# Two tiles' small products in one chain: grouping transposes, values and scores by kind

## The chip, the cores and the metric

The kernel runs on one core of a Trainium2 chip. The metric is the device time of one execution in microseconds, taken as the median of several runs. The profile tells of one profiled execution. Engines are called as the profile calls them: PE (TensorE, matmuls; PEld its weight loads), DVE (VectorE), ACT (ScalarE), POOL (GpSimd) and SP (SyncE, here a queue that issues transfers).

## The reference

Windowed attention with block summaries, and behind it an expert layer with a softmax gate and a layer norm. Cut to what matters:

```python
# q, k, v: 4 batches, 8 heads, 768 positions, 64 wide; blocks of 32, window 16
k_sum = k.reshape(B, H, nb, block, D).max(axis=3)
v_sum = v.reshape(B, H, nb, block, D).mean(axis=3)
scores_l = scale * q @ k.T                      # kept where |pos - pos'| < 16
scores_s = scale * q @ k_sum.T + log(block)
a = softmax(concat(masked scores_l, scores_s))
attn = a @ concat(v, v_sum)

x = attn as 3072 rows x 512
h = x @ w_in                                    # 512 x 1024
solu = h * softmax(h)
ln = (solu - mean) / sqrt(var + 1e-6) * g_ln
out = ln @ w_out                                # 1024 x 512
```

Everything is 32-bit. The two large products are made exact enough by splitting both operands into a high and a low part and adding three products of the parts.

## The kernel before, in words

The 3072 rows are 24 tiles of 128 rows (`NT`); tile `t` has two large products. `first(t)` makes h: 4 chunks of the contraction, two halves of 512 columns and three products each are 24 matmuls with 512 columns (line 706), into two PSUM banks that every tile from the third on uses again. `second(t)` makes o: 8 chunks and three products, 24 matmuls (line 784). Between the two the row statistics are made: the maximum (DVE, line 716), the exponential (ACT, 721), the product that reads h for the last time (DVE, 729), centring (737, 739 or 741), the sum of squares (ACT, 744) and the root (POOL, 748 to 756).

The attention before it is done in 24 steps, one for 4 heads (two of the four pairs of heads) and 256 positions; two steps, an even one and the odd one after it, make the x rows that two tiles read. Three kinds of small product belong to a step, all of them on PE:

- `scores` (S, line 587): 32 matmuls, 64 rows by 64 columns of the array, into PSUM. Ahead of them the keys are copied into windows (`kw`, 568 and 569). Behind them DVE masks and takes maxima (606), ACT takes exponentials with sums (614), and DVE or POOL multiplies by the inverse sum (621).
- `values_turn` (T): 16 transposes (line 642, tile `t`) of the weights `e`, and two copies to SBUF (`at`).
- `values` (V, line 681): 32 matmuls of `at` with the values (`vt`), and a copy and a subtraction that make the parts `xh` and `xl`.

A fourth kind belongs to a tile: `turn` (R), 16 transposes (line 642, tile `lt`) of its normed rows, with two copies (`lh`) and two subtractions (`ll`, line 769), so that `second` can use them as weights. R of tile t is done `LAG` - 1 = 3 tiles after its h, o of tile t is done 4 tiles after.

PSUM buffers: T, S and R (and a rare sum of values) share two slots with the tag `s`; V and o take turns in two banks (`place_x`). SBUF: `at`, `e`, `kw`, `qt`, `vt`, `lh` and `ll` have two buffers each, `he`, the rows of h, five (`NHE`).

The order is made by a planner (`Plan`) while the program is built. Every operation is recorded with its cost, the engines that can do it, and what it depends on through its buffers. `issue` gives each operation a due time, which for PE work is its place in the program, and `order` lists them greedily: the operation that can start first, and of several the one that is due first. It does this 64 times with noise on the due times and keeps the order with the earliest end on PE. Each engine then executes its list in that order. An operation with `then` set holds PE for its successor: nothing comes between.

From tile 6 on (`NEAR`) the main loop chains, in every tile t: T of step t + 3, then R of tile t - 3 together with V of step t + 2, then S of step t + 4. `run` records one or several generators as one operation on PE and lets each record what follows on the other engines. Up to tile 5 the small products are recorded one by one. The head of a chain also waits for what its second member waits for. `load_q`, `load_v` and `load_keys` are recorded at fixed places of the loop; `scored(i)` tells in which tile the scores of step i are made, and from it follows when keys are loaded and their block maxima taken.

Of the kernel before, what the change touches and what calls it, by code (L numbers as in the profile page):

```python
# [11 lines left out]
F32 = mybir.dt.float32  # L12
# [8 lines left out]
P = 128  # L21
# [5 lines left out]
QT = 64  # L27
# [10 lines left out]
NT = B * S // P  # L38
LAG = 4
NHE = 5  # L40
EARLY = 3
MEANS = 2
NEAR = 6
WPT = 2


# [26 lines left out]
class Plan:  # L73
# [41 lines left out]
    def op(self, engine, cost, fn, r=(), w=(), nbytes=0, after=(), alt=(), port=False):  # L115

        deps = set(after)

        def of(table, part):
            for k, v in table.items():
                if part is None or k is None or k == part:
                    deps.update(v)

        o = Op({e: (c, f) for e, c, f in ((engine, cost, fn), *alt)}, deps,
               len(self.ops), nbytes, port)
        r = [x if isinstance(x, tuple) else (x, None) for x in r]
        w = [x if isinstance(x, tuple) else (x, None) for x in w]
        for b, part in r:  # L130
            of(b.writers, part)
        for b, part in w:
            of(b.writers, part)
            of(b.readers, part)
            for p in b.prev:
                deps.update(p.ops)
                p.gone = True
        assert not any(b.gone for b, _ in r + w)
        for b, part in r:
            b.readers.setdefault(part, []).append(o)  # L140
            b.ops.append(o)
        for b, part in w:
            b.writers.setdefault(part, []).append(o)
            b.ops.append(o)
        deps.discard(o)
        self.ops.append(o)
        return o
# [115 lines left out]
def attn_then_solu(ctx: ExitStack, tc: tile.TileContext, q, k, v, vr, vb, w_in, w_out, g_ln, out):  # L263
# [3 lines left out]
    nc = tc.nc  # L267
    plan = Plan()
    op = plan.op
    pe, act, dve, pool, sp = "pe", "act", "dve", "pool", "sp"  # L270
# [12 lines left out]
    sb = ctx.enter_context(tc.tile_pool(name="sb", bufs=1))  # L283
# [150 lines left out]
    def load_keys(b, p, after=()):  # L434
        pp, i = divmod(p, 2)
        if i == 0:
            kraw[b, pp] = plan.buf(sb, [P, 2, SP], F32, "kraw", 3, f"kraw{b}_{pp}")
        x = kraw[b, pp]
        op(sp, 0.43, lambda: nc.sync.dma_start(out=x.ap[:, i], in_=k[b, pp, :, i]), w=[(x, i)], nbytes=P * SP * 4,
           after=after)  # L440

    def key_blocks(b, p):
        pp, i = divmod(p, 2)
        x = kraw[b, pp]
        if i == 0:
            ksum[b, pp] = plan.buf(sb, [P, 2, NB], F32, "ksum", 3, f"ksum{b}_{pp}")
        y = ksum[b, pp]
        op(dve, 0.87, lambda: nc.vector.tensor_reduce(
            out=y.ap[:, i], in_=x.ap[:, i, HALO:HALO + S].rearrange("p (n j) -> p n j", j=BLOCK),
            op=ALU.max, axis=AX.X), r=[(x, i)], w=[(y, i)])  # L450
# [82 lines left out]
    def load_q(b, g, pairs=None, after=()):  # L533
        if (b, g) not in qt:
            qt[b, g] = plan.buf(sb, [P, NPAIR, G * QT], F32, "qt", 2, f"qt{b}_{g}")
        x = qt[b, g]
        part = slice(None) if pairs is None else slice(2 * pairs, 2 * pairs + 2)
        op(sp, 0.43, lambda: nc.sync.dma_start(out=x.ap[:, part], in_=q[b, g, :, part]),
           w=[x] if pairs is None else [(x, 2 * pairs), (x, 2 * pairs + 1)],
           nbytes=P * 4096 if pairs is None else P * 2048, after=after)  # L540
# [81 lines left out]
           lambda: z.ap.rearrange("p (u o) -> p u o", o=1).broadcast_to([P, 8, KC]), r=[z], w=[e], port=True)  # L622
        es[b, g, pp] = e

    def run(*parts):

        mine = [x for x in ((f, next(f, None)) for f in parts) if x[1]]
        if mine:
            cost, fns, r, w = zip(*(x for _, x in mine))
            op(pe, sum(cost) - 0.25 * (len(mine) - 1), lambda: [f() for f in fns],  # L630
               r=[x for y in r for x in y], w=[x for y in w for x in y])
            done = plan.ops[-1]
        for f, _ in mine:
            assert next(f, None) is None
        return done if mine else None

# [7 lines left out]
    def values_turn(b, g, pp):  # L644
        nm_ = f"{b}_{g}_{pp}"
        e = es.pop((b, g, pp))

        tp = plan.buf(ps, [P, 2, 8, QT], F32, "s", 2, f"t{nm_}")
        yield 0.82, lambda: turn_halves(tp.ap[:KC], lambda n: e.ap[:, n, :]), [e], [tp]
        at = plan.buf(sb, [P, 2, 8, QT], F32, "at", 2, f"at{nm_}")  # L650
        for cu in range(2):
            copy(COPY_P, lambda cu=cu: at.ap[:KC, cu], lambda cu=cu: tp.ap[:KC, cu], r=[(tp, cu)], w=[(at, cu)])
        ats[b, g, pp] = at
# [105 lines left out]
    def turn(t):  # L759

        e = cen.pop(t)
        hi = plan.buf(sb, [P, NFC, P], F32R, "lh", 2, f"lh{t}")
        lo = plan.buf(sb, [P, NFC, P], F32R, "ll", 2, f"ll{t}")
        tp = plan.buf(ps, [P, 2, NFC, QT], F32, "s", 2, f"lt{t}")
        yield 0.85, lambda: turn_halves(tp.ap, lambda f: e.ap[:, f * P:(f + 1) * P]), [e], [tp]
        for r in range(2):
            part = lambda x, r=r: x.ap[:, :, r * QT:(r + 1) * QT]
            copy(COPY_P, lambda part=part: part(hi), lambda r=r: tp.ap[:, r], r=[(tp, r)], w=[(hi, r)])
            op(dve, 0.6, lambda part=part, r=r: nc.vector.tensor_tensor(  # L769
                out=part(lo), in0=tp.ap[:, r], in1=part(hi).bitcast(F32), op=ALU.subtract),  # L770
               r=[(tp, r), (hi, r)], w=[(lo, r)])
        lnT[t] = hi, lo
# [24 lines left out]
    its = [(b, g) for b in range(B) for g in range(NG)]  # L797
# [20 lines left out]
    for i in range(2 * NKC):  # L818
        split_w_in(*divmod(i, 2))
        if i % 2 == 0 and i < 2 * NPP:  # L820
            run(values_turn(0, 0, i // 2))
            run(values(0, 0, i // 2, 0, True))
# [6 lines left out]
        load_w(2 * NKC + f, w_out[f * P:(f + 1) * P, :])  # L829
    rows = [(hh, i) for hh in range(2) for i in range(2)]  # L830

    scored = lambda i: i - 2 if i - 2 < NEAR else max(NEAR - 1, i - 4)

    load_at, blocks_at = {}, {}
    for later in range(1, B):
        for p in range(NPAIR):
            t = scored(2 * NG * later + p // 2)
            old = 2 * NG * (later - 1) + (2 * NG - 2 if p > 1 else -1)
            free = scored(old) + (old - 2 >= NEAR) if old > 1 else 0
            load_at[later, p] = max(t - (3, 2, 2, 2)[p], free)  # L840
            blocks_at[later, p] = max(t - (2, 1, 2, 1)[p], load_at[later, p])

    def pairs(at, t):
        return [x for x in at if at[x] == t]

    step = lambda i: (*its[i // 2], i % 2)
    for t in range(NT):
        n, j = divmod(t, 2)
        b, g = its[n]
        near = t >= NEAR  # L850
        if not near:
            run(scores(*step(t + 2)))

        if t == NEAR - 1 or (near and j == 0 and n + 3 < len(its)):
            load_q(*its[n + 3])
        elif j == 0 and not near:
            load_q(*its[n + 2], after=begun if n == 0 else ())
        if j == 0 and n + 2 < len(its):
            load_v(*its[n + 2], after=begun if n == 0 else ())
        for p in pairs(load_at, t):  # L860
            load_keys(*p, begun if t < 4 else ())
        first(t)
        rows_behind = [turn(t - LAG + 1)] if t > LAG - 2 else []
        if near:
            parts = [run(values_turn(*step(t + 3)))] if t + 3 < NT else []
            parts.append(run(*rows_behind, *([values(*step(t + 2))] if t + 2 < NT else [])))
            if t + 4 < NT:
                parts.append(run(scores(*step(t + 4))))


            for x, y in zip(parts, parts[1:]):
                x.then = y
                y.deps.add(x)
            parts[0].deps.update(*[y.deps - {parts[0]} for y in parts[1:2]])
        else:
            run(*rows_behind)
        for f in range(WPT * t, min(WPT * t + WPT, NFC)):
            split_w_out(f)
        if t > LAG - 1:
            second(t - LAG)  # L880
        if not near:
            run(values_turn(*step(t + 2)))
            if t == NEAR - 1:
                run(scores(*step(t + 3)))
            run(values(*step(t + 2), t))
            if t == NEAR - 1:
                run(values_turn(*step(t + 3)))
                run(scores(*step(t + 4)))
        for p in pairs(blocks_at, t):
            key_blocks(*p)  # L890
        if t == MEANS:
            mean_values_pe(1)
        if 0 < b < B - 1 and g < 2:
            add_rows(b + 1, *rows[2 * g + j])
            if g == j == 1:
                mean_values(b + 1)
        if j == 1 and n + 2 < len(its):
            load_v2(*its[n + 2])
    for t in range(NT - LAG + 1, NT):
        run(turn(t))  # L900
        second(t - 1)
    second(NT - 1)

    def idle(x):
# [49 lines left out]
```

## Time and profile before

| | |
|---|---|
| median of 3 runs | 393.17 us (392.65 to 394.0) |
| span of the profiled execution | 392.1 us |
| PE busy | 383.5 us, 98% |
| PE weight loads | 298.3 us, 76% |
| DVE busy | 275.7 us, 70% |
| ACT busy | 248.7 us, 63% |
| POOL busy | 99.2 us, 25% |
| HBM read, written | 40.11 MB, 6.29 MB |

The page gives no whole-execution time for the profiled execution beside its span; the runs' median lies 1.07 us above the span. Times are from the first to the last instruction. Matmuls overlap: each large one is shown with about 0.39 us, but they start 0.23 us apart. So the rate of PE is read from starts, not from durations.

### The profile page before, as it was taken

To read this page: it belongs to the slowest core of one execution; us is meant where nothing else is said; L and a number is where in the kernel's file an instruction comes from. 1 tells how busy PE (TensorE), PEld (TensorE's weight loads), DVE (VectorE), ACT (ScalarE), POOL (GpSimd) and SP (SyncE) were. 2 spreads that over 40 slices of the span, in tenths; PEclk is the share of its full clock that TensorE was granted. 3 is DMA by queue.
4 is the path that set the end of the run, shared out by engine and by line. 5 is a ranking of instruction groups with operands and counts; after the bars stand their busy time and mean duration, and the time that the engine had idled before them with its cause. 6 is when DMAs were issued, how large, how long until landed. Compare 5 with 4: busy or idle time off the path is not lost.

```text
span 392.1 us, 9677 instructions
## 1 busy us (share of the span) xinstructions
PE 383.5 (98%) x3697; PEld 298.3 (76%) x3703; DVE 275.7 (70%) x884; ACT 248.7 (63%) x746; POOL 99.2 (25%) x245
## 2 busy tenths in 40 slices
PE   8999998999999999999999999999999999999996
PEld 3535766667878888878888888888888888888786
DVE  4999998999889877577767657667658664554330
ACT  3889686999798846657548557468467363533411
POOL 4325011515854421237220121220121021101100
PEclk9999999999999999999999999999999999999999
DMA  7999992136269230363330320330310000000011
GB/s 286 417 419 382 353 367 89 57 109 176 84 218 238 89 134 2 125 188 112 106 131 2 138 80 27 144 87 28 107 49 28 3 28 27 13 16 28 28 55 54
DMA packets 14994, 49.24 MB, mean 126 GB/s; under 512 B 1836, under 2 KB 2092, under 8 KB 13412
## 3 DMA queue, kind: packets, MB, share of 16 engines
q1 hardware_dynamic: 11084, 41.89, 30.8%
q10 hardware_dynamic: 3864, 6.74, 4.6%
q8 instruction: 29, 0.48, 0.5%
q14 instruction: 17, 0.14, 0.1%
HBM read 40.11 MB, written 6.29 MB: 118 GB/s over the span
## 4 chain that ended last, share of the span: by engine, by line
PE 81%; DMA 7%; DVE 6%; ACT 3%; issue 1%; ACTq 1%; SPq 0%; DVEq 0%
PE o L784 35%; PE h L706 29%; PE x L681 5%; PE s L587 4%; PE lt L642 3%; PE t L642 3%; DMA raw<-in_w_in 3%; DMA g_sb<-in_g_ln 2%; DMA vt<-vsum 1%; DMA qt<-in_q 1%; DVE e L606 1%; DVE cv L388 1%; DVE he L729 1%; ACT at L289 1%; DVE cv L296 1%
## 5 line engine op out<-in xcount | busy, mean ns | idle before, releaser
L784 PE MATMUL o<-w,lh 128*128 128x512 f32 (+1 forms) x400 | 127.2, 388 | 0.1
L706 PE MATMUL h<-w,xh 128*128 128x512 f32 x384 | 125.5, 394 | 0.4 <-DVE he L729 0.4
L614 ACT ACTIVATE e<-e,nm 128x120 f32<-128x120 f32 x192 | 73.1, 385 | 25.1 <-DVE nm L606 25.0
L784 PEld LDWEIGHTS o<-w,lh 128*128 128x128 f32 x400 | 74.1, 188 | 17.6 <-issue 2.4
L706 PEld LDWEIGHTS h<-w,xh 128*128 128x128 f32 x384 | 72.1, 188 | 17.5 <-ACT e L614 0.8
L784 PE MATMUL o<-w,ll 128*128 128x512 f32 (+1 forms) x200 | 76.4, 382 | 0.0
L706 PE MATMUL h<-w,xl 128*128 128x512 f32 x192 | 74.8, 390 | 0.0
L716 DVE TENSOR_REDUCE hm<-h 128x1 f32<-128x512 f32 x48 | 32.6, 686 | 40.4 <-PE h L706 40.4
L289 ACT COPY at<-t 120x512 f32<-120x512 f32 x46 | 24.8, 585 | 43.9 <-PE t L642 43.4
L784 PEld LDWEIGHTS o<-w,ll 128*128 128x128 f32 x200 | 37.7, 188 | 6.3
L706 PEld LDWEIGHTS h<-w,xl 128*128 128x128 f32 x192 | 36.0, 188 | 7.0
L606 DVE CUSTOM_DVE_ANT_0 e<-s,mask 128x120 f32<-128x120 f32 x192 | 40.6, 278 | 0.4 <-PE s L587 0.4
L721 ACT ACTIVATE he<-h,hm 128x512 f32<-128x512 f32 x48 | 32.8, 694 | 9.8 <-DVE hm L718 9.8
L614 ACT ACTIVATION_READ_ACCUMULATOR e<-e,nm 128x1 f32 x192 | 36.6, 191 | 0.0
L769 DVE TENSOR_TENSOR ll<-lt,lh 128x512 fp32r<-128x512 f32 x48 | 31.9, 683 | 5.8 <-ACT lh L289 5.6
L748 POOL TENSOR_SCALAR ss<-ss 128x1 f32<-128x1 f32 x24 | 7.1, 297 | 112.4 <-ACT sq L744 112.3
L729 DVE SCALAR_TENSOR_TENSOR he<-h,hz,he 128x512 f32<-128x512 f32 x48 | 34.1, 746 | 0.4
L681 PE MATMUL x<-at,vt 120*64 120x64 f32 (+1 forms) x768 | 28.3, 225 | 1.6 <-ACT at L289 1.6
L681 PEld LDWEIGHTS x<-at,vt 120*64 120x64 f32 (+1 forms) x768 | 24.6, 137 | 6.4 <-ACT at L289 2.9
L296 DVE TENSOR_TENSOR e<-e,z 128x960 f32<-128x960 f32 x23 | 26.6, 1156 | 0.5
L289 ACT CAST lh<-lt 128x512 fp32r<-128x512 f32 x33 | 18.6, 596 | 12.7 <-PE lt L642 9.7
L291 POOL COPY kw<-ksum 128x192 f32<-128x192 f32 x21 | 9.3, 445 | 65.8 <-PE s L587 33.4
(94 smaller groups left out, 519.0 us busy)
## 6 DMA issues: line engine op xcount, KB each, us to landing
vt<-in_v SPq DMA_DIRECT2D x12, 1024.0 KB, 5.4
kraw<-in_k SPq DMA_DIRECT2D x16, 400.0 KB, 9.4
out<-os ACTq DMA_DIRECT2D x23, 256.0 KB, 2.0
qt<-in_q SPq DMA_DIRECT2D x11, 512.0 KB, 5.1
raw<-in_w_in SPq DMA_DIRECT2D x8, 512.0 KB, 10.6
raw<-in_w_out SPq DMA_DIRECT2D x8, 512.0 KB, 9.2
st_v<-in_vr SPq DMA_DIRECT2D x6, 512.0 KB, 12.4
st_v<-in_vb SPq DMA_DIRECT2D x8, 384.0 KB, 3.2
```

What stands on the lines that cost most here:

```text
L289: by = {act: lambda: nc.scalar.copy(out=to(), in_=of()), dve: lambda: nc.vector.tensor_copy(out=to(), in_=of()), pool: lambda: nc.gpsimd.t ...
L296: by = {dve: lambda: nc.vector.tensor_tensor(out=to(), in0=a(), in1=b(), op=kind), pool: lambda: nc.gpsimd.tensor_tensor(out=to(), in0=a() ...
L606: nc.vector.tensor_tensor_reduce(out=e.ap[:, n, :], in0=sc.ap[:, j, (2 * i + up) * KC:(2 * i + up + 1) * KC], in1=mask[:, mi, :], scale=-S ...
L614: nc.scalar.activation(out=e.ap[:, n, :], in_=e.ap[:, n, :], func=AF.Exp, bias=nm.ap[:, n:n + 1], scale=-1.0, accum_out=z.ap[:, n:n + 1])
L642: nc.tensor.transpose(out=to[:, r, n, :], in_=of(n)[rows, :], identity=ident[rows, rows])
L681: nc.tensor.matmul(xp()[j * D:(j + 1) * D, i, qs], vs.ap[:k, u, cs], at.ap[:k, u % 2, n[j] + u // 2, :], start=not apart, stop=not apart o ...
L706: nc.tensor.matmul(hp.ap, a.ap[:, c, ts], w.ap[:, i], start=(c == 0 and n == 0), stop=(c == NKC - 1 and n == 2))
L716: op(dve, 0.6, lambda i=i, hp=hp: nc.vector.tensor_reduce(out=nms.ap[:, i:i + 1], in_=hp.ap, op=ALU.max, axis=AX.X, negate=True), r=[hp], ...
L721: op(act, 0.71, lambda i=i, hp=hp: nc.scalar.activation(out=part(i), in_=hp.ap, func=AF.Exp, bias=nm.ap, accum_out=zs.ap[:, i:i + 1]), r=[ ...
L729: op(dve, 0.67, lambda i=i, hp=hp: nc.vector.scalar_tensor_tensor(out=part(i), in0=hp.ap, scalar=zs.ap[:, 0:1], in1=part(i), op0=ALU.mult, ...
L769: op(dve, 0.6, lambda part=part, r=r: nc.vector.tensor_tensor(out=part(lo), in0=tp.ap[:, r], in1=part(hi).bitcast(F32), op=ALU.subtract), ...
L784: nc.tensor.matmul(o.ap[:, cols], a.ap[:, f, :], w.ap[:, i, cols], start=(f == 0 and n == 0), stop=(f == NFC - 1 and n == 2))
```

## The change

From tile 8 on (`PAIRED`) the small products of two tiles go together.

- In every even tile one chain holds T of steps t + 4 and t + 5, V of steps t + 2 and t + 3, and S of steps t + 6 and t + 7, in this order. Two blocks of one kind follow each other.
- The row transposes R of tiles t - 4 and t - 3 are a chain of two of their own, recorded ahead of `first(t)` of the even tile.
- The second T's copies are recorded after the first V (`rest=False`), and `at` has three buffers.
- At the end of tile 7 the deeper pipeline is filled: T of step 11 and S of steps 12 and 13 are recorded one by one.
- The head of a chain waits for what its first members wait for (two in the pair of R, three in the long chain), and for the PE work behind what the later ones wait for.
- The planner is told 0.25 us less for a block behind one of its kind (`off`).
- `load_q` goes to other places, `scored` changes with the scores, and so the keys of later batches are loaded in other tiles. In the tail the last four tiles' R are two pairs. The scratch for dynamic DMA is set to 8192.

```diff
+PAIRED = 8
...
-    def run(*parts):
+    def run(*parts, rest=True, off=0.0):
...
-            op(pe, sum(cost) - 0.25 * (len(mine) - 1), lambda: [f() for f in fns],
+            op(pe, sum(cost) - 0.25 * (len(mine) - 1) - off, lambda: [f() for f in fns],
                r=[x for y in r for x in y], w=[x for y in w for x in y])
             done = plan.ops[-1]
-        for f, _ in mine:
+        for f, _ in mine if rest else ():
             assert next(f, None) is None
...
-        at = plan.buf(sb, [P, 2, 8, QT], F32, "at", 2, f"at{nm_}")
+        at = plan.buf(sb, [P, 2, 8, QT], F32, "at", 3, f"at{nm_}")
...
-    scored = lambda i: i - 2 if i - 2 < NEAR else max(NEAR - 1, i - 4)
+    def scored(i):
+        if i < PAIRED + 4:
+            return i - 2 if i - 2 < NEAR else max(NEAR - 1, i - 4)
+        return PAIRED - 1 if i < PAIRED + 6 else i // 2 * 2 - 6
...
+    def chain(parts, first=2):
+
+        for x, y in zip(parts, parts[1:]):
+            x.then = y
+            y.deps.add(x)
+        mine = set(parts)
+        for x in parts[1:first]:
+            parts[0].deps.update(x.deps - mine)
+        for x in parts[first:]:
+            for d in x.deps - mine:
+                parts[0].deps.update([y for y in (d, *d.deps) if "pe" in y.can and y not in mine])
+
     for t in range(NT):
...
-        near = t >= NEAR
+        near, paired = t >= NEAR, t >= PAIRED
...
-        if t == NEAR - 1 or (near and j == 0 and n + 3 < len(its)):
+        if paired:
+            if t == PAIRED:
+                load_q(*its[n + 3])
+            if j and n + 4 < len(its):
+                load_q(*its[n + 4])
+        elif t == NEAR - 1 or (near and j == 0 and n + 3 < len(its)):
             load_q(*its[n + 3])
...
+        if paired and j == 0:
+            chain([run(turn(t - LAG)), run(turn(t - LAG + 1), off=0.25)])
         first(t)
-        rows_behind = [turn(t - LAG + 1)] if t > LAG - 2 else []
-        if near:
-            parts = [run(values_turn(*step(t + 3)))] if t + 3 < NT else []
-            parts.append(run(*rows_behind, *([values(*step(t + 2))] if t + 2 < NT else [])))
-            if t + 4 < NT:
+        if not paired:
+            rows_behind = [turn(t - LAG + 1)] if LAG - 2 < t < PAIRED - 1 else []
+            if near:
+                parts = [run(values_turn(*step(t + 3)))]
+                parts.append(run(*rows_behind, values(*step(t + 2))))
                 parts.append(run(scores(*step(t + 4))))
...
+                chain(parts)
+            else:
+                run(*rows_behind)
...
-        if t > LAG - 1:
+        if LAG - 1 < t < NT - 1:
             second(t - LAG)
...
+        if paired and j == 0:
+            parts = []
+            if t + 4 < NT:
+                behind = values_turn(*step(t + 5))
+                parts = [run(values_turn(*step(t + 4))), run(behind, rest=False, off=0.25)]
+            if t + 2 < NT:
+                parts.append(run(values(*step(t + 2))))
+                if t + 4 < NT:
+                    assert next(behind, None) is None
+                parts.append(run(values(*step(t + 3)), off=0.25))
+            if t + 6 < NT:
+                parts += [run(scores(*step(t + i)), off=0.25 * (i - 6)) for i in (6, 7)]
+            chain(parts, 3)
...
+        if t == PAIRED - 1:
+            run(values_turn(*step(t + 4)))
+            for i in (5, 6):
+                run(scores(*step(t + i)))
...
-    for t in range(NT - LAG + 1, NT):
-        run(turn(t))
+    for t in range(NT - LAG, NT, 2):
+        behind = turn(t + 1)
+        chain([run(turn(t)), run(behind, rest=False, off=0.25)])
         second(t - 1)
+        assert next(behind, None) is None
+        second(t)
     second(NT - 1)
...
-    nc = bacc.Bacc("TRN2", target_bir_lowering=False, num_devices=1)
+    nc = bacc.Bacc("TRN2", target_bir_lowering=False, num_devices=1, dynamic_dma_scratch_size=8192)
```

More of the change, by code (lines that the diff above doesn't have):

```diff
@@ L861, in attn_then_solu @@
             load_keys(*p, begun if t < 4 else ())
+        if paired and j == 0:
+            chain([run(turn(t - LAG)), run(turn(t - LAG + 1), off=0.25)])
         first(t)
-        rows_behind = [turn(t - LAG + 1)] if t > LAG - 2 else []
-        if near:
-            parts = [run(values_turn(*step(t + 3)))] if t + 3 < NT else []
-            parts.append(run(*rows_behind, *([values(*step(t + 2))] if t + 2 < NT else [])))
-            if t + 4 < NT:
-                parts.append(run(scores(*step(t + 4))))
[L871 to L876, printed above, removed]
+        if not paired:
[3 more added lines that the diff above has]
+                parts.append(run(*rows_behind, values(*step(t + 2))))
+                parts.append(run(scores(*step(t + 4))))
+                chain(parts)
+            else:
+                run(*rows_behind)
         for f in range(WPT * t, min(WPT * t + WPT, NFC)):
             split_w_out(f)
-        if t > LAG - 1:
+        if LAG - 1 < t < NT - 1:
             second(t - LAG)
```

## The prediction

> **What bounds the kernel now.** I read the page first, then the waits of TensorE, then its instructions in order of time across one steady period.
>
> ```profile
> span 392.1 us, 9677 instructions
> PE 383.5 (98%) x3697; PEld 298.3 (76%) x3703; DVE 275.7 (70%) x884; ACT 248.7 (63%) x746; POOL 99.2 (25%) x245
> PEclk9999999999999999999999999999999999999999
> PE x L681 <- ACT at L289: 1.6, 2, 1.0
> PE h L706 <- DVE he L729: 0.4, 1, 0.4
> ```
>
> TensorE is busy for 98% of the span, no slice falls below nine tenths of the clock, and the longest wait group of PE is 1.6 us in total. No transfer or other engine can give back much here; a gain has to come out of TensorE's own stream. So I read that stream (start, duration, instructions with their count):
>
> ```profile
> 204.30 0.39 PE L706 MATMUL h<-w,xh 128*128 128x512 f32 x1
> 204.62 0.69 PE L642 MATMUL t<-ident,e 64*120 64x64 f32 x16
> 205.15 0.66 PE L642 MATMUL lt<-ident,he 64*128 64x64 f32 x16
> 205.74 1.15 PE L681 MATMUL x<-at,vt 120*64 120x64 f32 x32
> 206.82 1.05 PE L587 MATMUL s<-kw,qt 64*64 64x120 f32 x32
> 207.80 0.50 PE L784 MATMUL o<-w,lh 128*128 128x512 f32 x1
> 208.14 0.40 PE L784 MATMUL o<-w,ll 128*128 128x512 f32 x1
> 208.37 0.62 PE L784 MATMUL o<-w,lh 128*128 128x512 f32 x2
> ...
> 218.90 0.69 PE L642 MATMUL t<-ident,e 64*120 64x64 f32 x16
> ```
>
> This is tile 12, counting the groups of 24 h matmuls. A period runs from 204.62 to 218.90: 14.28 us. The 48 large matmuls follow each other at 0.23 us (208.14 to 208.37; 0.227 over the long stretches), 10.88 us; the remaining 3.40 us are the small products with what their neighbourhood costs. Blocks, from start to the next start: T (values' transposes, t) 0.53, R (row transposes, lt) 0.59, V 1.08, S 0.98. The first large one after them takes 0.34 (207.80 to 208.14) instead of 0.23, with the next two slow as well: 0.13 in all; the step from the last h to T is 0.32 instead of 0.23: 0.09. 0.09 + 0.53 + 0.59 + 1.08 + 0.98 + 0.13 = 3.40.
>
> What a change of kind costs is read from the block's end. Single small matmuls last:
>
> ```profile
> L681 PE MATMUL x<-at,vt 120*64 120x64 f32 x704 | 25.6, 225 | 1.6 <-ACT at L289 1.6
> L587 PE MATMUL s<-kw,qt 64*64 64x120 f32 x704 | 23.1, 269 | 0.4 <-DVE ll L769 0.4
> L642 PE MATMUL t<-ident,e 64*120 64x64 f32 x384 | 16.5, 226 | 0.1
> ```
>
> T's last one starts at 204.62 + 0.69 - 0.23 = 205.08, R's first at 205.15: 0.06 between two blocks of transposes (rounded). V's last starts at 206.66 and S begins at 206.82: 0.15. S's last starts at 207.60, o begins at 207.80: 0.19. Inside blocks the mean step is 0.03. So leaving a block for another shape costs 0.12 (V) or 0.16 (S) over the ordinary step, and a seam between two transposes only 0.03.
>
> **The change, part by part.** The small work itself stays the same; what changes is how often TensorE changes its shape. I add up TensorE's time for everything small from tile 7 on, both ways.
>
> Before: tiles 7 to 19 have a full chain of T, R, V, S: 13 x 3.40 = 44.20. Tile 20 lacks S: 2.42. Tile 21 has R and V, and then R stands alone five times. Two rows give a lone R and a lone T:
>
> ```profile
> 117.28 0.69 PE L642 MATMUL t<-ident,e 64*120 64x64 f32 x16
> 117.89 0.50 PE L784 MATMUL o<-w,lh 128*128 128x512 f32 x1
> ...
> 346.24 0.71 PE L642 MATMUL lt<-ident,he 64*128 64x64 f32 x16
> 346.88 0.50 PE L784 MATMUL o<-w,lh 128*128 128x512 f32 x1
> ```
>
> A lone R costs 0.64 + 0.09 + 0.13 = 0.86, five of them 4.30; tile 21 0.09 + 0.64 + 1.08 + 0.13 = 1.94. Sum before: 52.86.
>
> After, tile 7: its chain has lost R (it waits for the pair at tile 8): 0.09 + 0.62 (lone T) + 1.08 + 0.98 + 0.13 = 2.90. Once, T of step 11 and S of 12 and 13 are issued by themselves to fill the deeper pipeline: 0.62 + 0.22 = 0.84 and 2 x (0.98 + 0.22) = 2.40, together 3.24. Tiles 8, 10, 12, 14, 16: T T V V S S. The T T seam is the one measured; V V and S S stand nowhere in the trace. Bounds: nothing saved (each block as long as today), or the whole of leaving and entering a shape, 0.19 (S's 0.16 plus T's 0.03 slower start: led by h, T takes 0.53; following T, R takes 0.59 with an exit of 0.15 in it against 0.06). I take the excess of leaving, 0.12 for V and 0.16 for S, since the nearest row, the T R seam, shows it nearly gone: 0.09 + 0.53 + 0.59 + (2.16 - 0.12) + (1.96 - 0.16) + 0.13 = 5.18, five times 25.90. Tile 18 (T T V V): 3.38. Tile 20 (V V): 2.26. Ten pairs of row transposes, each 0.09 + 0.53 + 0.59 + 0.13 = 1.34, stand alone: 13.40. Sum after: 51.08. **TensorE's stream becomes 1.78 us shorter.** Of this the steady pair gives 6.80 - 5.18 - 1.34 = 0.28, five times 1.4; the tail and tile 7 give about 1.5, and the three single blocks, dearer alone than in a chain, take about 1.1 back. With nothing saved at V V and S S (seven and five seams, 1.64 us) 0.14 would be left; with 0.19 at all twelve it is 2.4.
>
> [...]
>
> **What hides the rest.** These I cost at nothing, each by its cover. The second T's copies to SBUF must wait until the first V has read its third buffer, and the second S needs the PSUM slot that they free: V + S, 2.06 us, lie between; both halves take 1.07 us on ACT today (below). The second V takes the bank of the o just finished, whose eviction (0.75, below) has T T V, 2.20 us. The row transposes of a tile now precede its own o by one tile's h (5.5 us) instead of two large groups and more; the copies and subtractions need about 2.0 us (0.60 and twice 0.69). If another instruction stands before one of these, up to 1.5 us of exponentials, they still fit. The SP queue: a query load is issued two steps further ahead and the keys of batches 2 and 3 some tiles earlier; they pass value loads whose slots are free by then, and a landing of 5.1 or 9.4 us has at least one tile (over 11 us) before its scores. Nobody waits on SP itself. [...]
>
> ```profile
> q1 hardware_dynamic: 11084, 41.89, 30.8%
> kraw<-in_k SPq DMA_DIRECT2D x16, 400.0 KB, 9.4
> qt<-in_q SPq DMA_DIRECT2D x11, 512.0 KB, 5.1
> ```
>
> **Handover at tile 7.** Here one dependent path runs: S 11, its softmax, T 11, its copies, S 13 (the same two PSUM slots and e buffers), its reduction, then the first R pair, its copies, o of tile 4. Before, S 11 ended at 135.10 and its e was ready at 143.68:
>
> ```profile
> 132.65 1.07 ACT L289 COPY at<-t 120x512 f32<-120x512 f32 x2 [1.26 <-PE t L642]
> 135.10 0.50 PE L784 MATMUL o<-w,lh 128*128 128x512 f32 x1
> 137.83 0.28 DVE L606 CUSTOM_DVE_ANT_0 e<-s,mask 128x120 f32<-128x120 f32 x1
> 138.16 0.40 ACT L614 ACTIVATE e<-e,nm 128x120 f32<-128x120 f32 x1 [0.88 <-DVE nm L606]
> 140.83 0.38 ACT L614 ACTIVATE e<-e,nm 128x120 f32<-128x120 f32 x1
> 140.87 0.75 DVE L791 TENSOR_SCALAR os<-o,y 128x512 f32<-128x512 f32 x1
> 142.52 1.16 DVE L296 TENSOR_TENSOR e<-e,z 128x960 f32<-128x960 f32 x1
> L606 DVE CUSTOM_DVE_ANT_0 e<-s,mask 128x120 f32<-128x120 f32 x192 | 40.6, 278 | 0.4 <-PE s L587 0.4
> L769 DVE TENSOR_TENSOR ll<-lt,lh x4: 682/684/689, 209.0 to 226.4; 128x512 fp32r<-128x512 f32 x4
> L289 ACT CAST lh<-lt x2: 587/596/605, 207.6 to 222.9; 128x512 fp32r<-128x512 f32 x2
> ```
>
> That is 8.6 us, of which 2.7 were waiting for DVE; without waits about 5.4. The path: 5.4 to 8.6, T 0.62, copies 1.07, S 0.98, reduction 1.7 (40.6 for 24 of them), R 0.53, copies 2.0, seven handoffs, estimated at 0.1 each (the first exponential follows the reduction's first piece, ended at 138.11, by 0.05): 13 to 16.2, and 17.2 if each of three insertions waits half a large block. TensorE's own work in it: o of tile 3 (5.6), the three single blocks 3.24, h of tile 8 (5.5), the R pair 1.34: 15.7. So it waits 0 to 1.5 us; I take 0.3, since the planner puts the earliest due first and S 11 is due next.
>
> **Sum.** -1.78 + 0.3 = -1.48 us. The span of 392.1 becomes 390.6. The median of the runs, 393.17, is 1.1 us above the span; nothing in the change touches what lies around it. Prediction 391.7.
>
> **Rivals.** First, the seams save nothing (V V and S S cost what a change costs): gain 0.14 less 0.3, 393.3. For it: no row shows them. Against it: T R shows 0.06. Second, the handover costs more, because softmaxes of steps 11, 12 and 13 crowd on DVE and ACT together: 1.2 to 3 us, so 392.6 to 394.4, about 393.2. For it: DVE started the reduction 2.7 us late even with one softmax. Third, the planner places the single blocks beside their like: 1.1 us more gained, 390.6.
>
> Fourth, on the other side: **the h banks**. Only two PSUM banks hold h; the next tile may start when VectorE has multiplied the last. Today o and a whole chain lie between any two h. Afterwards, from an odd tile to an even one, only o and the R pair: from the last h's end 0.23 - 0.39 + 5.44 + 0.09 + 1.14 = 6.5 us. What it takes now:
>
> ```profile
> 211.29 0.75 DVE L729 SCALAR_TENSOR_TENSOR he<-h,hz,he 128x512 f32<-128x512 f32 x1
> ...
> 218.58 0.39 PE L706 MATMUL h<-w,xh 128*128 128x512 f32 x1
> 223.47 0.74 DVE L729 SCALAR_TENSOR_TENSOR he<-h,hz,he 128x512 f32<-128x512 f32 x1
> ```
>
> Tile 12's h ended at 204.69, its first bank was free at 212.04: 7.35. Tile 13's at 218.97 and 224.21: 5.24. The first had a reduction of scores (eight instructions) ahead of it. If the odd tiles take 7.35, each of the six boundaries from 9 to 20 loses 0.85, 5.1 in all: 396.8. It decides from 6.9 on (6 x 0.4 cancels the gain and adds 0.9). Against it: a pair's two reductions and eight of its sixteen exponentials fit into the 5.5 us of h itself, and at the h's end no row transposes compete, which they do today. I price it at half the loss, 394.3 to 396.8, middle 395.3. [...]
>
> **Chances.** Forecast 0.52 (391.7, its own range 390.9 to 392.5: seams and handover); seams without gain 0.08; handover 0.18; joined blocks 0.10; h banks 0.12. About 0.3%, 1.2 us, can be told from no change here, so the line is at 392.0. Forecast: 0.36 faster, 0.16 same. Joined blocks: faster. Seams: same. Handover: 0.14 same, 0.04 slower. Banks: 0.03 same, 0.09 slower. Faster 0.46, same 0.41, slower 0.13. The range goes from 390.4 (joined blocks) to 395.0, leaving out the worse half of the banks' case.
>
> **What the profile after would show.** In the steady part: V V about 2.04 instead of 2 x 1.08, S S 1.80, a period of two tiles of 28.28 instead of 28.56 us, ten lone pairs of lt of about 1.12 us. A wait of PE before o of tile 4 of 0.3 us; none over 0.4 on he (L729) before an even tile's h. Wrong it would be if waits of PE named he L729, ll L769 or at L289 with several us, or if the first stretch up to tile 6, whose order the planner also draws anew, moved by over 1 us.

## The result, and the profile after

The changed kernel took 396.75 us (median of 4 runs, 395.6 to 397.82) against 393.01 us before: a ratio of 1.010, 95% interval 1.0084 to 1.0115. It is 3.7 us slower; 391.7 had been predicted, with a range up to 395.0. Three of the four runs after show a granted clock of 0.995 or 0.996; the profiled one, with 1.000, is the shortest of them (its span lies 1.7 us below its time). Which run the profile before belongs to is not recorded; its span of 392.1 and the same 1.7 us make 393.8, near the longest of its runs (394.0) and 0.8 us above the median. So the two profiles show less of a difference, 1.8 us, than the medians do.

The page after, and what PE waited for:

```profile
span 393.9 us, 9712 instructions
PE 381.7 (97%) x3705; PEld 296.7 (75%) x3705; DVE 263.0 (67%) x858; ACT 262.2 (67%) x769; POOL 102.4 (26%) x248
PE vs_ps L469 <- DMA st_v<-in_vr: 1.9, 1, 1.9
PE t L643 <- DVE e L297: 1.4, 1, 1.4
...
PE x L682 <- ACT at L290: 0.9, 2, 0.7
PE o L785 <- DVE ll L770: 0.8, 1, 0.8
PE h L707 <- DVE he L730: 0.7, 1, 0.7
```

PE is busy 1.8 us less than before, in a span that is 1.8 us longer: the work did shrink, and waits took its place. Before, no single wait of PE was longer than the 1.24 us at the program's start; now two are longer, one far ahead of the change (the values' rows at 22 us) and one at tile 7. The steady part, in order of time:

```profile
188.62 1.16 PE L643 MATMUL t<-ident,e 64*120 64x64 f32 x32
189.72 2.09 PE L682 MATMUL x<-at,vt 120*64 120x64 f32 x64
191.73 1.87 PE L588 MATMUL s<-kw,qt 64*64 64x120 f32 x64
193.53 0.50 PE L707 MATMUL h<-w,xh 128*128 128x512 f32 x1
```

```profile
204.64 1.21 PE L643 MATMUL lt<-ident,he 64*128 64x64 f32 x32
...
216.90 0.81 PE L643 MATMUL t<-ident,e 64*120 64x64 f32 x20
```

This is very nearly the forecast: T T 1.10, V V 2.01, S S 1.80 (each from its start to the next start), and two tiles in 216.90 - 188.62 = 28.28 us instead of 28.56. The loss is elsewhere. From the first h of tile 7 to the last matmul (starts) the rows before and after say:

```profile
126.39 0.39 PE L706 MATMUL h<-w,xh 128*128 128x512 f32 x1
...
388.75 0.28 PE L784 MATMUL o<-w,lh 128*128 128x256 f32 x1
```

```profile
126.94 0.39 PE L707 MATMUL h<-w,xh 128*128 128x512 f32 x1
...
390.52 0.28 PE L785 MATMUL o<-w,lh 128*128 128x256 f32 x1
```

262.36 us before, 263.58 after. Taking PE's steps from one start to the next, what they take beyond the usual step between the same two kinds adds up to 0.0 before and 2.6 after: 1.5 ahead of the chain of tile 7, 1.1 in o of tile 4. Without them the stretch would be 1.4 us shorter. What delayed tile 7's chain stands on VectorE, eleven microseconds earlier:

```profile
122.10 0.21 DVE L733 TENSOR_SCALAR nmu<-s 128x1 f32<-128x1 f32 x1
125.22 0.95 DVE L449 TENSOR_REDUCE ksum<-kraw 128x24 f32<-128x768 f32 x1 [2.91 <-DMA kraw<-in_k]
```

```profile
133.97 0.42 PE L643 MATMUL t<-ident,e 64*120 64x64 f32 x7 [1.43 <-DVE e L297]
```

DVE stood 2.91 us waiting for a key load of batch 3 whose maxima nobody needs before tile 12. The softmax of step 10 stood behind it in DVE's list, and PE behind the softmax.

### The profile page after: what moved, and what is told of

It is laid out like the page before. It is cut to its first block, busy times and chain, and to the rows that moved or that the text cites. A ratio compares the mean times of both kernels' runs of the same rounds, so it can differ in the third digit from the quotient of the medians.

```text
span 393.9 us, 9712 instructions
## 1 busy us (share of the span) xinstructions
PE 381.7 (97%) x3705; PEld 296.7 (75%) x3705; DVE 263.0 (67%) x858; ACT 262.2 (67%) x769; POOL 102.4 (26%) x248
## 3 DMA queue, kind: packets, MB, share of 16 engines
q1 hardware_dynamic: 11084, 41.89, 30.3%
q10 hardware_dynamic: 3864, 6.74, 4.6%
## 4 chain that ended last, share of the span: by engine, by line
PE 63%; ACT 5%; DMA 3%; DVE 2%; POOL 1%; issue 0%; ACTq 0%; DVEq 0%
PE o L785 29%; PE h L707 22%; PE x L682 4%; PE s L588 3%; PE lt L643 3%; DMA kraw<-in_k 3%; ACT e L615 2%; PE t L643 2%; DVE ll L770 1%; ACT he L742 1%; POOL st_v L511 1%; ACT kw L290 1%; ACT at L290 1%; PE vs_ps L526 1%; DVE e L607 0%
## 5 line engine op out<-in xcount | busy, mean ns | idle before, releaser
L707 PE MATMUL h<-w,xh 128*128 128x512 f32 x384 | 127.8, 399 | 0.7 <-DVE he L730 0.7
L785 PE MATMUL o<-w,lh 128*128 128x512 f32 (+1 forms) x400 | 125.8, 385 | 0.3 <-DVE w L412 0.3
L607 DVE CUSTOM_DVE_ANT_0 e<-s,mask 128x120 f32<-128x120 f32 x192 | 40.3, 277 | 6.3 <-PE s L588 6.3
L770 DVE TENSOR_TENSOR ll<-lt,lh 128x512 fp32r<-128x512 f32 x48 | 30.5, 685 | 20.1 <-ACT lh L290 20.0
L749 POOL TENSOR_SCALAR ss<-ss 128x1 f32<-128x1 f32 x24 | 6.1, 254 | 116.7 <-ACT sq L745 114.1
L742 ACT ACTIVATE he<-he,nmu 128x512 f32<-128x512 f32 x27 | 19.1, 722 | 24.0 <-DVE nmu L733 23.9
L790 ACT ACTIVATE os<-o,y 128x512 f32<-128x512 f32 (+1 forms) x21 | 13.9, 664 | 26.5 <-PE o L785 22.2
L290 ACT CAST lh<-lt 128x512 fp32r<-128x512 f32 x45 | 23.6, 592 | 10.4 <-PE lt L643 10.4
L682 PE MATMUL x<-at,vt 120*64 120x64 f32 (+1 forms) x768 | 26.8, 225 | 0.9 <-ACT at L290 0.9
```

The source lines that it names most:

```text
L290: by = {act: lambda: nc.scalar.copy(out=to(), in_=of()), dve: lambda: nc.vector.tensor_copy(out=to(), in_=of()), pool: lambda: nc.gpsimd.t ...
L607: nc.vector.tensor_tensor_reduce(out=e.ap[:, n, :], in0=sc.ap[:, j, (2 * i + up) * KC:(2 * i + up + 1) * KC], in1=mask[:, mi, :], scale=-S ...
L682: nc.tensor.matmul(xp()[j * D:(j + 1) * D, i, qs], vs.ap[:k, u, cs], at.ap[:k, u % 2, n[j] + u // 2, :], start=not apart, stop=not apart o ...
L707: nc.tensor.matmul(hp.ap, a.ap[:, c, ts], w.ap[:, i], start=(c == 0 and n == 0), stop=(c == NKC - 1 and n == 2))
L742: (act, 0.57, lambda sl=sl: nc.scalar.activation(out=e.ap[:, sl], in_=e.ap[:, sl], func=AF.Identity, bias=nmu.ap))], port=True)
L785: nc.tensor.matmul(o.ap[:, cols], a.ap[:, f, :], w.ap[:, i, cols], start=(f == 0 and n == 0), stop=(f == NFC - 1 and n == 2))
```

## The experiments

Each was timed beside the kernel before on the same chip (three chips in all; medians of 392.6 to 392.9 us for the kernel before). A figure such as 1.0105 (1.0085 to 1.0125) is the ratio to it with its 95% interval. "Draw" is the seed among the planner's 64: it chose 8 for the kernel before and 42 for the changed one.

**The draw alone, on both kernels.**

```diff
-        for seed in range(self.TRIES):
+        for seed in (42,):          # e1, in the kernel before; (8,) in e2, in the changed one
```

> The kernel before, with one thing changed: the planner takes its draw 42, the one it chose for the changed kernel, instead of draw 8. Up to the middle of tile 4 the order on every engine is then that of the changed kernel. Theory A (the early order, drawn anew, costs most of what was lost): 1.5 to 2.5 us slower than the kernel before, 394.5 to 395.5, with a granted clock of about 0.995 in most runs, as three of four runs of the changed kernel had. Theory B (the pairing itself, from tile 7 on, costs it): within 0.6 us of the kernel before, clock 1.000.

Measured: 396.79 us, 1.0105 (1.0085 to 1.0125). The kernel before, unpaired, with nothing but the other draw, is as slow as the changed one (396.75 in the result, 395.56 when timed again beside it, e4). The draw costs more than theory A expected, and not by the clock: four of five runs had 0.999 or 1.000. The wait at 22 us is there (the row below); tile 7's first h came at 128.17 instead of 126.39. Another 1.2 us come behind that (263.53 us from there to the last matmul against 262.36), so e1 prices the whole draw and not the early order alone.

```profile
PE vs_ps L468 <- DMA st_v<-in_vr: 1.9, 1, 1.9
```

> The changed kernel with the planner's draw 8, that of the kernel before: the same order up to tile 4 or 5 as before. Theory A: the loss goes; what is left is the seams' gain of about 1.6 us less the handover's waits of 1 to 2.6 us: 392.4 to 394.0, clock 1.000. Theory B: 396 or more, as with draw 42.

Measured: 395.64 us, 1.0072 (1.0057 to 1.0087), missed. The early loss did go: tile 7's first h at 125.07 (the row below). The first h of tiles 0 and 4 show where the loss had been, in e2 (the first pair of rows) and in the changed kernel with draw 42 (the second pair):

```profile
125.07 0.39 PE L707 MATMUL h<-w,xh 128*128 128x512 f32 x1
```

```profile
38.26 0.50 PE L707 MATMUL h<-w,xh 128*128 128x512 f32 x1
...
80.23 0.39 PE L707 MATMUL h<-w,xh 128*128 128x512 f32 x1
```

```profile
37.14 0.50 PE L707 MATMUL h<-w,xh 128*128 128x512 f32 x1
...
82.00 0.39 PE L707 MATMUL h<-w,xh 128*128 128x512 f32 x1
```

With draw 42 tile 0 begins 1.1 us earlier, in spite of the wait at 22 us, and then needs 44.86 us to tile 4 instead of 41.97. In the first 80 us the kernel issues matmuls on zeros where its plan leaves PE idle; seven of them, which e2 does not have at this place, fill 1.67 us:

```profile
55.11 1.69 PE L947 MATMUL t<-zero 128*128 128x512 bf16 x7
```

So the early order loses between tiles 0 and 4. The wait at 22 us is not what it loses against e2, save where the clock falls behind it (e4).

But a new loss came at tile 8, with a clock of 0.995 or 0.996 in all five runs. The second row transposes of the first pair, and the clock there (columns: stretch, its length, busy time of PE, PEld, DVE, ACT and POOL, granted clock, DMA):

```profile
147.54 0.71 PE L643 MATMUL lt<-ident,he 64*128 64x64 f32 x16
150.42 0.71 PE L643 MATMUL lt<-ident,he 64*128 64x64 f32 x16 [2.18 <-DVE hz L725]
```

```profile
146.00:151.00 5.00, 2.82 (x67) 2.18 (x65) 4.93 (x24) 3.71 (x14) 1.15 (x1) 1.00 0.44 157
151.00:155.00 4.00, 3.68 (x14) 2.85 (x10) 3.25 (x8) 4.00 (x15) 1.36 (x2) 0.57 0.01 2
```

PE holds for the PSUM slot of S 13: the row names the instruction that stands behind S 13's reduction in DVE's list, and the reduction (L607) runs from 148.58 to 150.28. Right behind that wait TensorE runs at half clock for 3.4 us (0.57 over the 4 us of the second row; large matmuls start 0.43 us apart there, at 152.04 and 152.47, instead of 0.23).

**The key maxima held back.** The orders on PE and SP stay the same as in the changed kernel. (From e6 on the condition reads `t >= 8`, the same tile.)

```diff
-            key_blocks(*p)
+            key_blocks(*p, after=[o for o in plan.ops if "pe" in o.can][-1:] if t >= PAIRED else ())
```

> The changed kernel, draw 42, but the block maxima of the keys of batch 3 (two reductions that DVE stood waiting for at 122 to 125 us) may not start before tile 10. The orders on PE and SP stay the same. Theory C (VectorE, waiting in order for a key load that lands late, delays step 10's softmax and with it the chain of tile 7): 1.4 us faster than the changed kernel, about 395.3, and no wait of PE for e at 132 us. Rival: the chain waits for something else anyway, time unchanged at about 396.7.

> The changed kernel again, unaltered, on the same chip as the three others: 396 to 397.5, most runs with a clock of about 0.995. If the profiled run is one of these, its clock row shows where in the span the half-speed stretch lies; theory A expects it in the first 40 us, where PE waits 1.9 us for the values' rows.

Measured: e3 394.69 us (1.0064, 1.004 to 1.0089), e4 395.56 us (1.0072, 1.0051 to 1.0093). The hold gives 0.9 us by the medians where 1.4 was expected; in e4's own profile the wait for e was 0.95 us, not 1.43, and in e3 it is gone from PE's list, so theory C holds. e4 had only one run of six with a low clock, not most; it is the profiled one:

```profile
20.00:22.00 2.00, 0.00 (x0) 0.00 (x0) 2.00 (x4) 2.00 (x12) 0.00 (x0) 1.00 1.03 420
22.00:26.00 4.00, 3.84 (x6) 0.79 (x6) 3.69 (x8) 2.79 (x6) 0.00 (x0) 0.57 1.03 425
```

PE had nothing for 2.2 us, and then 3.4 us at half clock (0.57 over the 4 us of the second row). Tile 0's first h came at 39.19 instead of 37.14 us.

**The row transposes ahead of the single blocks, without and with held keys, and pairs from tile 10.**

```diff
         if t == PAIRED - 1:
+            chain([run(turn(t + 1 - LAG)), run(turn(t + 2 - LAG), off=0.25)])
             run(values_turn(*step(t + 4)))
...
-        if paired and j == 0:
+        if t > PAIRED and j == 0:
             chain([run(turn(t - LAG)), run(turn(t - LAG + 1), off=0.25)])
```

> The changed kernel, draw 8, with the first pair of row transposes (tiles 4 and 5) recorded at the end of tile 7 ahead of the three single blocks instead of behind them, so that it no longer needs the PSUM slot of the scores of step 13. Theory D (the handover's chain of dependences, S 13 to its reduction to the row transposes to o of tile 4, makes PE wait 2.2 us and drop to half clock for 3.4 us): both go, 3 to 4.5 us faster than the same draw unmended, 391.2 to 392.7, clock 1.000 in all runs. Rival (the three softmaxes at once are too much for DVE and ACT whatever the order): the wait moves to the chain of tile 8, 394.5 to 396.

Measured: 396.81 us (1.0094, 1.007 to 1.0118): failed. The wait for S 13's slot is gone, but the key loads now stop DVE for 3.1 us, and PE waits longer than in any other kernel for e:

```profile
PE t L643 <- DVE e L297: 3.2, 1, 3.2
DVE ksum L449 <- DMA kraw<-in_k: 3.1, 2, 2.8
```

> As e5_rows_first, and the block maxima of batch 3's keys held until tile 10 as in e3_keys_held. With both, 8 is also the draw that the planner's 64 tries choose by themselves. Theory D with C: 390.8 to 392.3, faster than the kernel before by 0.15 to 0.5%. Rival: 394.5 or more.

Measured: 392.94 us (1.0011, 1.0002 to 1.002), 3.9 us below e5 by the held maxima alone. All twelve runs had a clock of 0.999 or 1.000, while four of e5's six had 0.990 to 0.996; e5's two others took 394.69 and 395.45 us, so some 2 us are the wait and the rest goes with the clock. It is 0.6 us short of the expectation.

> As e6_rows_and_keys, but the pairs begin at tile 10 instead of tile 8, where DVE and ACT have finished with the second product's weights. One steady pair fewer (0.28 us). If the handover still costs something in e6 because DVE and ACT are full around 135 us, this one is equal or faster, 390.5 to 392; if nothing is left there, 0.3 us slower than e6.

Measured: 392.45 us (0.9992, 0.9983 to 1.0001): slightly faster than e6, so something was left at the handover. From tile 7 on e6 still waits, longest here:

```profile
157.94 1.05 PE L588 MATMUL s<-kw,qt 64*64 64x120 f32 x32
159.84 1.05 PE L588 MATMUL s<-kw,qt 64*64 64x120 f32 x32 [0.85 <-DVE at L291]
```

```profile
156.38 0.49 DVE L740 TENSOR_SCALAR he<-he,nmu 128x512 f32<-128x512 f32 x1
159.00 0.69 DVE L291 COPY at<-t 120x512 f32<-120x512 f32 x1 [2.14 <-ACT at L290]
```

```profile
157.27 0.73 ACT L742 ACTIVATE he<-he,nmu 128x512 f32<-128x512 f32 x1
157.90 0.58 ACT L290 CAST xh<-x 128x512 fp32r<-128x512 f32 x1
158.36 0.61 ACT L290 COPY at<-t 120x512 f32<-120x512 f32 x1
```

The second S waits for the second T's two copies. ACT makes one at 158.36, behind two other instructions; DVE, idle for 2.14 us, starts the other at 159.00, only when ACT has ended its own. Put on two engines, the halves came one after the other, which the planner counts as parallel; why DVE's half waited for ACT's is not shown.

**The early wait filled.**

```diff
             def mm(i=i, x=x):
+                for _ in range(10 if i == 0 else 0):
+                    nc.tensor.matmul(acc.ap, zero[:, :P], zero[:, :512], start=True, stop=True)
                 for c in (2 * i, 2 * i + 1):
```

> The changed kernel, draw 42, with ten idle matmuls of 0.22 us on PE just ahead of the first sums of values, where PE waits 1.9 to 2.2 us for a load; the orders elsewhere are the same. Theory E (this early idle stretch lets the clock fall to half for 3.4 us in part of the runs, 2 us each time): no run with a clock below 0.999, and the spread of the runs shrinks to 394.3 to 395.6. Rival (the dips have another cause): runs at 0.994 to 0.996 and 396.5 to 398 remain.

Measured: 395.49 us (1.0072, 1.0053 to 1.0091), no run of six below 0.999. No dip came, as theory E says, but six runs do not prove it: of the 33 runs with draw 42 and without these matmuls (the result, e1, e3, e4, e12) 12 had a clock of 0.996 or less, so that six without one would come by luck about once in 15. And one run still took 396.76 us: the spread has another part.

**The second T's copies on one engine.**

```diff
-                behind = values_turn(*step(t + 5))
+                behind = values_turn(*step(t + 5), ((dve, 0.6),))   # costs of both copies
```

> As e6_rows_and_keys (pairs from tile 8, row transposes first, key maxima held, draw 8), and both halves of the second T's copies go to DVE instead of one to ACT and one to DVE. The orders on PE and SP stay the same. Theory F (the waits that are left in e6, 0.85 us at the second S of tile 8's chain and 0.1 to 0.3 us in each later one, come from the two halves: DVE starts its half only when ACT has ended the other, behind two more ACT instructions, while DVE stood idle): about 1.3 us faster than e6, 391.4 to 391.9. Rival (DVE is then late for xl and the reductions, and the wait moves on): 392.5 to 393.2.

Measured: 391.44 us, 0.9964 (0.9951 to 0.9976): 0.36% faster than the kernel before, clear of its interval, as theory F expected. The chain of tile 8 runs through, DVE making both copies at 158.25:

```profile
157.06 2.09 PE L682 MATMUL x<-at,vt 120*64 120x64 f32 x64
159.07 1.87 PE L588 MATMUL s<-kw,qt 64*64 64x120 f32 x64
160.87 0.50 PE L707 MATMUL h<-w,xh 128*128 128x512 f32 x1
```

```profile
158.25 1.29 DVE L291 COPY at<-t 120x512 f32<-120x512 f32 x2 [0.27 <-PE x L682]
```

From the first h of tile 7 to the end it takes 260.95 us against 262.36 before: 1.41 less, with 0.5 of waits left.

> As e8_paired_10 with the same edit. Theory F: 0.4 us faster than e8 (its waits at the second S are 0.2 to 0.35 us in each of three chains), 391.9 to 392.3. Rival: unchanged, 392.3 to 392.6.

Measured: 391.81 us (0.998, 0.9967 to 0.9992), 0.1 better than the expectation. With the handover mended, tile 8 is the better place: from the first h of tile 7 to the last matmul e10 takes 261.79 us, e9 260.95.

**The two controls.** e11 is e2 with the key maxima held; e12 is e9 with draw 42.

> The changed kernel, draw 8, with batch 3's key maxima held, but the first pair of row transposes where the change has it. It parts the two mends of e6: held keys alone. Theory D (the row transposes behind the scores of step 13 make PE wait 2 us and fall to half clock): still 1.5 to 3 us slower than e6, 394.5 to 396, with runs at a clock of 0.995. Rival (the key maxima were the whole cause at the handover): within 0.5 us of e6, 392.5 to 393.4, clock 1.000.

Measured: 400.02 us (1.0177, 1.0156 to 1.0198). The direction is theory D's, the size twice what it expected. The pair of row transposes waits for S 13's slot, o of tile 4 for the copies, and the clock is at half for about 6.9 us, worked out from the 0.62 and the 0.52 of two stretches of 4 us:

```profile
150.88 0.72 PE L643 MATMUL lt<-ident,he 64*128 64x64 f32 x16 [2.15 <-DVE hm L719]
153.03 0.80 PE L785 MATMUL o<-w,lh 128*128 128x512 f32 x1 [1.43 <-DVE lh L291]
```

```profile
151.00:155.00 4.00, 2.05 (x19) 1.30 (x19) 2.65 (x4) 4.00 (x19) 0.00 (x0) 0.62 0.01 2
155.00:159.00 4.00, 4.00 (x11) 3.12 (x10) 3.90 (x9) 0.68 (x3) 0.00 (x0) 0.52 0.00 0
```

> e9_second_copies_dve with the planner's draw 42 instead of 8: all three mends of the handover, but the early order of the changed kernel. Theory A, as far as it stands after e1: the early order alone costs 2 to 3.5 us, so 393.5 to 395, slower than the kernel before, with a dip of the clock at 22 us in some runs. Rival (the handover was the whole loss and the draw's cost in e1 belonged to the unpaired kernel): within 0.8 us of e9, 390.7 to 392.2.

Measured: 393.75 us (1.003, 1.0011 to 1.0049), 2.3 us above e9: the early order's price on a kernel without the handover's waits. Five of twelve runs had a clock of 0.996; the median of the other seven is 392.65, so without the dips the price is 1.2 us. From tile 7 on the two need nearly the same (261.19 us against 260.95). Over all profiles, tile 7's first h came at 124.8 to 126.4 us with draw 8 (eight profiles, median 125.1) and at 126.0 to 128.9 with draw 42 (six, median 127.5).

## Why the prediction was wrong, point by point

**The seams were right.** V V 2.01 (2.04 predicted), S S 1.80 (1.80), the period 28.28 (28.28). The stream without waits became 1.4 us shorter (1.78), and in e9 the whole stretch by 1.41, close to the predicted 1.48. The far bound, nothing saved, is refuted, and so is the first rival: V V took 2.01 us, less than 2 x 1.08.

**The step that failed first is a term that the sum does not have: the stretch up to tile 6.** I added up TensorE's time "from tile 7 on", so that the stretch ahead of it counted as unchanged, and named the planner's new order only as a sign of being wrong, at the very end and without a price. The planner picks its draw anew for every program, and draw 42 orders even the first tiles otherwise. It cost 3.9 us on the kernel before (e1) and 2.3 us on the mended one (e12), as much as or more than the change could gain. I could have bounded it: the seed, the noise and the plan's own times were all in the code.

**The key loads' zero failed.** I weighed the landing against the scores that need it and said nobody waits on SP. True, but the maxima stand in DVE's list, and while one of them waited, nothing behind it in the list ran: 2.91 us on DVE, 1.43 on PE; 3.2 on PE in e5. The question I left out was who is queued behind the instruction that waits.

**The handover's term was mis-sized.** The path was named rightly (S 13, its reduction, the row transposes, o of tile 4). I took 0.3 us of a range of 0 to 1.5; the changed kernel shows 2.6 in that region, 1.5 of it by the keys and 1.1 on the path, within my range, and with draw 8 the path itself made PE wait 2.2 us (e2) and 3.6 us (e11). The second rival was right in kind, at 1.2 to 3 us, but I gave it 0.18. That a wait can also cost the clock, 3.4 us at half behind 2.2 us in e2, was in none of the terms.

**The cover of the second S held in the changed kernel (0.2 us in one chain) but not in every order.** In e6 it cost 0.85 us at tile 8, since the copies were split between engines and ran in turn.

**The fourth rival was wrong.** Tile 11, an odd one:

```profile
198.88 0.39 PE L707 MATMUL h<-w,xh 128*128 128x512 f32 x1
```

```profile
202.95 0.75 DVE L730 SCALAR_TENSOR_TENSOR he<-h,hz,he 128x512 f32<-128x512 f32 x1
```

Its first bank was free 203.70 - 199.27 = 4.4 us after h's end, against 6.5 available, and PE's one wait for he (0.7 us on the page) is at 99 us, ahead of the change. So at this place the emptying of PSUM did not hold PE up; at the handover's PSUM slots PE did wait for it, 2.18 us in e2, 0.85 in e6 and 2.15 in e11.

The 3.7 us in sum, from single profiles that differ by about 1 us: the early order 1.9 (tile 7's first h at 126.94 against 125.07 in e2), waits 2.6, dips of the clock 1.15 (the median run over the profiled one), seams -1.4: 4.2. The profile before itself reached tile 7 1.3 us later than e2, with the same order up to tile 4: at 66 us PE waits 1.03 us there for ACT's copies `at` (part of the row of 1.6 us that the prediction shows). The profile of e9 has this wait too, 1.01 us, e2's does not; e9's profile is of the longest of its runs, and the profile before seems to be too. What brings it, and what else spreads the runs in e7, is open. No run shows what the smaller scratch costs, for which the sum has no term: it was not tried alone; the two hardware_dynamic queues show 11084 and 3864 packets before and after.

## What to carry to other kernels

Where a planner or a random search orders the program, an edit can change the draw that is chosen, and with it the order far ahead of the edit: compare on a fixed draw before judging the edit, and give the redraw a price of its own in a forecast. An instruction that waits for a transfer can be paid by what stands behind it in its engine's list (here 2.91 us of DVE on a key load became 1.43 us of PE), so early work that nobody needs yet is not free. When a pipeline is deepened, follow the one dependent path through the tile where the depth changes; the steady state said nothing about it.

## What the runs showed of the hardware

A wait of PE of about 2 us cost twice in three of the profiles. In e4 2.19 us without work, up to 22.16 us, were followed by 3.4 us at half clock, and tile 0's first h came 2.05 us later than in the profile of the changed kernel; in e2 2.18 us up to 150.42 by the same, and all five runs had a clock of 0.995 or 0.996; in e11 a wait of 2.15 us up to 150.88, with one of 1.43 up to 153.03 soon behind it, went with about 6.9 us at half.

It did not always come: an early wait of 1.88 us left the profiled run of the changed kernel at full clock, and so did 3.2 us in the profiled run of e5, which lie in this row (columns as in e2's):

```profile
128.00:134.00 6.00, 2.81 (x25) 2.11 (x25) 4.41 (x11) 5.01 (x21) 2.28 (x4) 1.00 0.11 44
```

So the length of the wait alone does not tell in these traces whether the clock falls behind it: 3.2 us had no dip, 2.2 us had one. What decides it is not shown.
